# Loading part of one block without its padding rows: two 48-row transfers and engine fills in place of one 128-row transfer

## The chip, the cores and the metric

The kernel runs on one core of one Trainium2 chip. The metric is the device time of one execution in microseconds (us). The kernel before was timed in three runs: 544.09, 544.38 and 549.07 us, median 544.38 us. A further execution was recorded by the profiler; it took 545.84 us, of which 544.1 us lie between its first and its last instruction (the span).

## What is computed

An attention-like recurrence over four batches, eight heads, 768 steps and a head width of 48, and after it a dense layer with an elementwise function.

```
for t in range(S):                       # S = 768, heads of D = 48
    cur   = einsum('bhd,bhe->bhde', u * k[t], v[t])
    y[t]  = einsum('bhd,bhde->bhe', r[t], state + cur)
    state = w[t][:, :, :, None] * state + einsum('bhd,bhe->bhde', k[t], v[t])
x = y.transpose(0, 2, 1, 3).reshape(3072, 384)
h = x @ w_in                             # 384 x 2048
out = (h - tanh(h)) @ w_out              # 2048 x 384
```

## The kernel before, in words

The 3072 tokens are cut into eight blocks of 384 tokens (batch b, half q of the sequence). For each block the kernel first does the recurrence in chunks of 64 steps, and then the dense layer in 16 steps of 128 hidden columns. The recurrence of a block runs beside the dense layer of the block ahead of it; only the first block has nothing to run beside. It is done by the function boot (L1128), which stands at the very start. The change lies in boot alone.

Two heads share one tile of 128 rows: head 0 of a pair takes rows 0 to 47, head 1 takes rows 64 to 111, and rows 48 to 63 and 112 to 127 are padding (1.0 for w, 0.0 for k and r, from the host). There are four pairs. A block's half is two pairs: HALVES is (2, 0), so h1 is pairs 2 and 3, and h2 is pairs 0 and 1. The second half, h2, is what the change touches. For one half, w is a tile of 128 x 780 numbers (two pairs of six chunks of 65), k and r are 128 x 768. In the profile the tile of w of the first block is called states, since it lies in the buffer states0.

All loads of boot go out from one queue, SyncE's (SP), one after the other, through load (L361) and load_v (L401): w of pair 3, w of pair 2, k of h1, r of h1, w of h2, v of all four pairs, k of h2, r of h2, and then weights ("raw", 768 KB each, L251). The order on each engine is that in which the code is written, for PE, SP, VectorE (DVE) and ScalarE (ACT) alike (manual_schedule, L1102). Each transfer takes one of eight completion counters in turn, and in the emitted program a transfer waits until the one eight before it has landed.

What the steps of boot do, with the lines by which the profile names them:

- behind (L429) scans w backwards into post, before (L417) scans it forwards into pre; take_whole (L449) picks the decay of each chunk; both scans are on DVE.
- times_behind (L443, DVE) multiplies k into post; times_before (L436, DVE) multiplies r into pre; times_u (L454, ACT) multiplies k by u in place.
- own and earlier are gram products on PE (L494); their results are copied into the tile scores under a mask (L502, DVE). turn_1 (L517) transposes post on PE, turn_2 (L523, ACT) copies it out.
- update_half (L616, PE), states_half (L631, L632, DVE), from_scores (L697, PE), from_states (L679, PE) and result_out (L729) make the states and the block's result xT. The first dense step starts with L871 on PE.
- convert (L264 on ACT, L268 on DVE) makes fp32 weights of a raw tile.

On VectorE boot goes: behind and take_whole of h1, before, times_behind and times_before of h1, behind and take_whole of h2 (L429, L449), own of h1 (L502), times_behind of h2 (L443), earlier of h1 (L502), and so on. So the h2 scan L429 is the first user of w of h2, the L443 after it the first user of k of h2, and the second L436 the first user of r of h2.

Ahead of boot, VectorE fills the tiles shift (L152) and seed (L163, L164), GpSimd (POOL) makes ident and the tile start, which is 128 x 780 zeros (L171), and ScalarE copies zeros from start into scores (L205) and first_totals (L294). PE is kept busy with matmuls that nobody reads (L305, L312).

Of the kernel before, what the change touches and what calls it, by code (L numbers as in the profile page):

```python
# [50 lines left out]
B, H, S, D = 4, 8, 768, 48  # L51
P = 128
L = 64
NB = 384
NQ = S // NB
NCH = NB // L
NCP = NCH // 2
NPAIR = H // 2
LP = L + 1
WIDE = NPAIR * NCH * LP  # L60
HALF = WIDE // 2 + 2
UP = 2
# [64 lines left out]
def kernel(  # L127
# [12 lines left out]
    nc = tc.nc  # L140
# [29 lines left out]
    start = const.tile([P, UP * NCH * LP], F32, name="start", tag="start")  # L170
# [16 lines left out]
    def draw(names, cols):  # L187
        nc.gpsimd.memset(mask_all[0:L, cols], 1.0)
        for m in names:
# [5 lines left out]
            else:  # L195
# [10 lines left out]
                   in_=start[:, 0:BANK].unsqueeze(1).to_broadcast([P, 2 * NPAIR * NCP * L // BANK, BANK]))  # L206
# [46 lines left out]
    def convert(part, j, raw, _, tiles=1):  # L253

        lo, hi = raw[:, :, 0], raw[:, :, 1]
        a = w_sb[:, part, 2 * j:2 * j + 2].rearrange("p f c -> p (f c)").bitcast(I32)
        up = conv.tile([P, 2 * DM], I32, name="up", tag="up", bufs=4)
        low, high = (up.bitcast(t).rearrange("p (n two) -> p n two", two=2)[:, :, i]  # L260
                     for i, t in enumerate((U16, F16)))

        def scaled(to, of, scale, bias=0.0):
            return lambda: nc.scalar.activation(out=to, in_=of, func=AF.Copy, scale=scale, bias=bias)  # L264

        return [scaled(a.bitcast(F32), hi.bitcast(F32), HIGH_SCALE), scaled(high, hi.bitcast(F32), SIGN_SCALE),
                scaled(low, lo.bitcast(U32), *LOW)], [
                lambda of=slice(i * 2 * DM // tiles, (i + 1) * 2 * DM // tiles): nc.vector.scalar_tensor_tensor(  # L268
                    out=a[:, of], in0=a[:, of], scalar=3, in1=up[:, of], op0=ALU.logical_shift_left,
                    op1=ALU.bitwise_or) for i in range(tiles)]  # L270
# [43 lines left out]
    def begin_behind(ins, then):  # L314
        tc.add_manual_dep(then.ins, ins.ins.name, mybir.DependencyInfo(
            mybir.DependencyClass.Sync, mybir.DependencyReason.DATA))
# [3 lines left out]
    class Block:  # L320
# [37 lines left out]
                self.tot = work.tile([P, NPAIR * NCH], F32, name="whole", tag="whole")  # L358
            return self.tot[:, p0 * NCH:(p0 + n) * NCH]

        def load(self, name, p0=0, n=NPAIR, as_=None):  # L361
            as_ = as_ or name
            if name == "w":
                dst = self.tile(name)[:, p0 * NCH * LP:(p0 + n) * NCH * LP]
                src = wT[self.b, p0:p0 + n, :, self.q * NCH * LP:(self.q + 1) * NCH * LP]
            else:
                dst = self.tokens(as_, p0, n)
                src = {"r": rT, "k": kT}[name][self.b, p0:p0 + n, :, self.cols]
            return nc.sync.dma_start(out=dst.rearrange("d (p t) -> d p t", p=n),
                                     in_=src.rearrange("p d t -> d p t"))  # L370

        def by_token(self, name):

# [133 lines left out]
        def own(self, ps, p0, **fill):  # L507
            return self.masked(ps, "k", "r", masks["diagonal"], p0, **fill)

        def earlier(self, ps, p0, **fill):  # L510
            return self.masked(ps, "post", "pre", masks["above"], p0, **fill)
# [593 lines left out]
    def more_weights(queue):  # L1105
        raws.append(load_weights(more_weights.n, queue))
        more_weights.n += 1
        return raws[-1][-1]
# [3 lines left out]
    def run(ops):  # L1112
        for op in ops:
            op()
# [13 lines left out]
    def boot(ps, pair, blk, later):  # L1128
        h1, h2 = HALVES
        blk.tiles["w"] = states0  # L1130
        for name, p0, n in (("w", h1 + 1, 1), ("w", h1, 1), ("k", h1, UP), ("r", h1, UP), ("w", h2, UP)):
            blk.load(name, p0, n)
        blk.load_v()
        blk.load("k", h2, UP)
        blk.load("r", h2, UP)
        more_weights(nc.sync)

        both = (h1, h1 + 1), (h2, h2 + 1)
        blk.behind(h1 + 1, 1)
        blk.behind(h1, 1)  # L1140
        blk.take_whole(h1, UP)
        blk.totals_by_column(h1)
        nc.scalar.copy(out=later_ident, in_=ident)
        blk.before(h1, UP)
        blk.times_behind(h1, UP)
        blk.times_u(h1, UP)
        own = blk.own(ps, h1, spare=94, ahead=5, late=6)
        blk.turn_1(ps, h1)
        blk.times_before(h1, UP)
        earlier = blk.earlier(ps, h1)  # L1150
        blk.behind(h2, UP)
        blk.take_whole(h2, UP)
        first_a, first_b = convert(*raws.pop(0), tiles=2)
        own()
        blk.turn_2(h1)
        blk.totals_by_column(h2)
        blk.update_half(pair, h1)
        begin_behind(blk.done, more_weights(nc.sync))
        blk.times_behind(h2, UP)
        blk.times_u(h2, UP)  # L1160
        blk.turn_1(ps, h2)
        blk.turn_2(h2)
        earlier()
        blk.results(ps)
        blk.result("from_scores", both[0])
        run(blk.states_half(h1))
        blk.result("from_states", both[0], True, apart=True)
        blk.before(h2, UP)
        blk.update_half(pair, h2)
        blk.times_before(h2, UP)  # L1170
        own = blk.own(ps, h2)
        own_scored = blk.done
        run(first_a[:1])
        blk.result_out((3,), [nc.scalar.copy] * 2)
        blk.result_out((2,))
        earlier = blk.earlier(ps, h2, ahead=1)
        scored = blk.done
        onwards = blk.states_half(h2)
        own()
        run(first_a[1:])  # L1180
        needed = 2 * KC - 2
        blk.fill_holes([nc.sync, nc.gpsimd], range(needed, 2 * KC))
        begin_behind(own_scored, more_weights(nc.sync))
        blk.fill_holes([nc.sync, nc.gpsimd], range(needed))
        begin_behind(scored, more_weights(nc.sync))
        later.load("w")
        second_a, second_b = convert(*raws.pop(0))
        third_a, third_b = convert(*raws.pop(0))
        run(second_a)
        more_weights(nc.sync)  # L1190
        blk.results(ps)
        blk.yp.reverse()
        blk.result("from_states", both[1], apart=True)
        earlier(1, 1)
        earlier(0, 1)
        for p in reversed(both[1]):
            blk.result("from_scores", (p,), True, more=True)
        later.load("k")
        more_weights(nc.sync)
        run(onwards)  # L1200
        run(first_b[:1])
        for p in reversed(both[1]):
            blk.result_out((p,), [nc.scalar.copy, nc.vector.tensor_copy])
        run(first_b[1:])
        run(third_a[:2])
        run(second_b)
        blk.held(0, NPAIR)
        return [(third_a[2], third_b)]
# [6 lines left out]
    with tc.tile_pool(name="ps_boot", bufs=1, space=PSUM) as ps_boot:  # L1215
        pieces = boot(Turns([scratch(ps_boot)] + ps_a.both), [hp] + acc, blocks[0], blocks[1])
# [30 lines left out]
    for i, blk in enumerate(blocks):  # L1247
# [9 lines left out]
        for f in range(NF):  # L1257
# [60 lines left out]
            if not later and f == NF - 2:  # L1318
                at = n_whole + n_excess
# [29 lines left out]
            for name in loads.get(f, ()):  # L1349
                of, ins = (after if name in ("w", "k", "r") else later), None  # L1350
                if name == "weights":
                    ins = more_weights(nc.sync)
                elif name == "row":
                    ins = nc.sync.dma_start(out=u_row, in_=u_all)
                elif of and name.startswith("tokens"):
                    ins = of.load_tokens(name[-1])
                elif of:
                    ins = of.load_v() if name == "v" else of.load(name.split()[-1])
# [95 lines left out]
```

## Time and profile before

| what | value |
|---|---|
| three runs | 544.09, 544.38, 549.07 us |
| profiled execution, of that its span | 545.84 us, 544.1 us |
| VectorE, ScalarE busy | 459.0 us (84%), 403.8 us (74%) |
| DMA moved | 56.34 MB, mean 104 GB/s |
| mean granted TensorE clock | 0.995 |

The profile is one execution. Its page gives busy time per engine, and the chain of work that ended last, which is followed back from the last instruction. The timeline lists instructions by start (us from the span's start) and duration; a square bracket gives the idle time of the engine just before and what ended it. For a transfer the trace has the time of its issue on the queue and the time from the start of that issue until it has landed. The windows view gives for stretches of time the busy time of each engine, the granted TensorE clock, the mean busy share of the 16 DMA engines and what they moved.

### The profile page before, as it was taken

To read this page: it belongs to the slowest core of one execution; us is meant where nothing else is said; L and a number is where in the kernel's file an instruction comes from. 1 tells how busy PE (TensorE), PEld (TensorE's weight loads), DVE (VectorE), ACT (ScalarE), POOL (GpSimd) and SP (SyncE) were. 2 spreads that over 40 slices of the span, in tenths; PEclk is the share of its full clock that TensorE was granted. 3 is DMA by queue.
4 is the path that set the end of the run, shared out by engine and by line. 5 is a ranking of instruction groups with operands and counts; after the bars stand their busy time and mean duration, and the time that the engine had idled before them with its cause. 6 is when DMAs were issued, how large, how long until landed. Compare 5 with 4: busy or idle time off the path is not lost.

```text
span 544.1 us, 14866 instructions
## 1 busy us (share of the span) xinstructions
PE 533.7 (98%) x5682; PEld 404.1 (74%) x5682; DVE 459.0 (84%) x943; ACT 403.8 (74%) x814; POOL 6.6 (1%) x47
## 2 busy tenths in 40 slices
PE   7899999999999999999999999999999999999996
PEld 5756666678887788777877787877878787787874
DVE  7889999999989989789897979879897997457564
ACT  5799996888668876688676886588866885666561
POOL 1100000000000000000000000000000000000000
PEclk9899999999999999999999999999999999999999
DMA  7798633251402631154212532137231420200101
GB/s 274 236 400 308 237 102 115 87 146 60 121 19 79 159 110 54 58 128 138 60 55 73 121 116 67 49 89 161 67 97 54 92 56 2 57 1 0 45 1 46
DMA packets 53048, 56.34 MB, mean 104 GB/s; under 512 B 21488, under 2 KB 50928, under 8 KB 52976
## 3 DMA queue, kind: packets, MB, share of 16 engines
q1 hardware_dynamic: 52592, 55.18, 33.8%
q8 instruction: 48, 0.79, 0.6%
q14 instruction: 24, 0.20, 0.1%
q10 hardware_dynamic: 288, 0.10, 0.1%
q0 software_dynamic: 96, 0.07, 0.1%
HBM read 44.73 MB, written 4.72 MB: 91 GB/s over the span
## 4 chain that ended last, share of the span: by engine, by line
PE 95%; DVE 2%; issue 1%; DMA 0%; PEld 0%; PEldq 0%; DVEq 0%; SPq 0%
PE hp L871 44%; PE acc L999 26%; PE att L999 7%; PE acc L950 5%; PE att L757 4%; PE att L494 2%; PE acc L977 2%; PE att L575 1%; PE att L871 1%; PE acc L871 1%; DVE post L429 1%; DVE scores L502 1%; DMA states<-in_wT 0%; DVE pre L417 0%; PE att L977 0%
## 5 line engine op out<-in xcount | busy, mean ns | idle before, releaser
L871 PE MATMUL hp<-xT,w_sb 128*128 128x384 f32 x738 | 259.2, 487 | 0.4 <-DVE w_sb L268 0.4
L871 PEld LDWEIGHTS hp<-xT,w_sb 128*128 128x128 f32 x738 | 131.9, 190 | 69.7 <-issue 0.5
L999 PE MATMUL acc<-forms,g 128*128 128x128 f32 x954 | 133.2, 276 | 0.0
L876 ACT ACTIVATE h<-hp 128x384 f32<-128x384 f32 x123 | 60.4, 491 | 97.3 <-PE hp L871 97.1
L999 PEld LDWEIGHTS acc<-forms,g 128*128 128x128 f32 x954 | 122.0, 192 | 10.3
L879 DVE SCALAR_TENSOR_TENSOR h<-h,s 128x384 f32<-128x384 f32 x128 | 70.5, 551 | 50.5 <-ACT s L894 50.4
L920 DVE TENSOR_TENSOR g<-g 128x256 f32<-128x256 f32 x265 | 103.1, 418 | 7.3 <-PE acc L999 6.5
L895 ACT ACTIVATE qa<-s,shift 128x384 f32<-128x384 f32 x113 | 69.5, 615 | 3.7
L897 ACT ACTIVATE junk<-s,shift 128x384 bf16<-128x384 f32 x113 | 67.7, 599 | 0.0
L879 DVE SCALAR_TENSOR_TENSOR g<-qa,h 128x384 f32<-128x384 f32 x112 | 61.6, 550 | 1.6 <-ACT qa L905 0.2
L894 ACT ACTIVATE s<-h 128x384 f32<-128x384 f32 x113 | 59.1, 523 | 3.5
L999 PEld LDWEIGHTS acc<-w_sb,g 128*128 128x128 f32 x318 | 46.8, 191 | 9.7 <-ACT sums L967 0.3
L999 PE MATMUL acc<-w_sb,g 128*128 128x128 f32 x318 | 53.1, 276 | 0.0
L999 PE MATMUL att<-w_sb,g 128*128 128x128 f32 x212 | 35.5, 275 | 0.0
L999 PEld LDWEIGHTS att<-w_sb,g 128*128 128x128 f32 x212 | 31.1, 192 | 5.3
L1034 DVE TENSOR_TENSOR sums<-sums 128x256 f32<-128x256 f32 x84 | 32.8, 406 | 1.7 <-ACT sums L1011 1.5
L950 PE MATMUL acc<-w_sb,sums 128*128 128x384 f32 x96 | 33.7, 487 | 0.0
L264 ACT ACTIVATE up<-raw 128x768 f16<-128x768 f32 (+1 forms) x32 | 33.1, 1069 | 0.0
L950 PEld LDWEIGHTS acc<-w_sb,sums 128*128 128x128 f32 x96 | 18.0, 190 | 12.3 <-DVE sums L879 0.3
L417 DVE TENSOR_TENSOR_SCAN pre<-w,start 128x780 f32<-128x780 f32 x14 | 25.0, 1783 | 0.8
L429 DVE TENSOR_TENSOR_SCAN post<-w,seed 128x780 f32<-128x780 f32 x14 | 24.8, 1774 | 0.0
L897 ACT ACTIVATION_READ_ACCUMULATOR junk<-s,shift 128x1 f32 x113 | 21.1, 187 | 0.0
(118 smaller groups left out, 529.2 us busy)
## 6 DMA issues: line engine op xcount, KB each, us to landing
raw<-in_weights SPq DMA_DIRECT2D x16, 768.0 KB, 5.9
w<-in_wT SPq DMA_DIRECT2D x7, 780.0 KB, 4.6
k<-in_kT SPq DMA_DIRECT2D x7, 768.0 KB, 4.6
r<-in_rT SPq DMA_DIRECT2D x7, 768.0 KB, 4.6
v_sb<-in_v SPq DMA_DIRECT2D x8, 576.0 KB, 3.9
k<-in_tokens SPq DMA_DIRECT2D x7, 576.0 KB, 5.2
r<-in_tokens SPq DMA_DIRECT2D x7, 576.0 KB, 4.7
out_y<-sums SPq DMA_DIRECT2D x18, 128.0 KB, 1.8
```

Of the source, the lines that this page charges most:

```text
L264: return lambda: nc.scalar.activation(out=to, in_=of, func=AF.Copy, scale=scale, bias=bias)
L429: return nc.vector.tensor_tensor_scan(out=back(t[:, 0:width]), data0=back(self.tile("w")[:, a:a + width]), data1=back(seed[:, 0:width]), i ...
L871: nc.tensor.matmul(hp, lhsT=w_in_sb[:, f, kc, :], rhs=xT[kc], start=(kc == KC - 1), stop=(kc == 0))
L876: return h, nc.scalar.activation(out=h, in_=hp, func=AF.Copy, scale=1.0 / UPSCALE)
L879: return lambda: nc.vector.scalar_tensor_tensor(out=out, in0=in0, scalar=scalar, in1=in1, op0=op0, op1=ALU.mult)
L894: nc.scalar.activation(out=s, in_=h, func=AF.Square)
L895: nc.scalar.activation(out=qa, in_=s, func=AF.Square, bias=shift[:, 4:5])
L897: nc.scalar.activation(out=junk[:, 0:NB], in_=s, func=AF.Relu, bias=shift[:, 5:6], accum_out=excess[:, at:at + 1])
L920: return lambda: nc.vector.tensor_tensor(out=G[:, to:to + 2], in0=two(G, g_at(q, a0), g_at(q, a1)), in1=two(G, g_at(q, b0), g_at(q, b1)), ...
L950: nc.tensor.matmul(acc, lhsT=g[:, j * P:(j + 1) * P], rhs=w_out_sb[:, f, :], start=(f == self.first), stop=(f == NF - 1))
L999: nc.tensor.matmul(to, lhsT=G[:, g_at(q, a), :], rhs=rhs, start=start, stop=stop, skip_group_check=True)
L1034: ops.append(lambda op=op, at=at: nc.vector.tensor_tensor(out=at[0], in0=at[1], in1=at[2], op=OPS[op]))
```

## The change

load gets an argument rows, a list of row ranges, and issues one transfer for each. In boot, w, k and r of h2 are loaded for rows 0 to 47 and then for rows 64 to 111. The padding rows come from fills of the whole half tile, which are issued before these loads: w with 1.0 and k with 0.0 on VectorE, r on ScalarE by a copy from the tile of zeros. In the emitted program the fill of w stands on VectorE between the two fills of seed, the fill of k behind them and ahead of the first scan; the copy on ScalarE stands behind L294. Each of the first transfers of w, k and r waits for its fill.

```diff
-        def load(self, name, p0=0, n=NPAIR, as_=None):
+        def load(self, name, p0=0, n=NPAIR, as_=None, rows=(slice(0, P),)):
...
-            return nc.sync.dma_start(out=dst.rearrange("d (p t) -> d p t", p=n),
-                                     in_=src.rearrange("p d t -> d p t"))
+            for at in rows:
+                ins = nc.sync.dma_start(out=dst[at].rearrange("d (p t) -> d p t", p=n),
+                                        in_=src[:, at].rearrange("p d t -> d p t"))
+            return ins
...
     def boot(ps, pair, blk, later):
...
-        for name, p0, n in (("w", h1 + 1, 1), ("w", h1, 1), ("k", h1, UP), ("r", h1, UP), ("w", h2, UP)):
+        filled = slice(0, D), slice(64, 64 + D)
+        for name, p0, n in (("w", h1 + 1, 1), ("w", h1, 1), ("k", h1, UP), ("r", h1, UP)):
             blk.load(name, p0, n)
+        nc.vector.memset(blk.tile("w")[:, h2 * NCH * LP:(h2 + UP) * NCH * LP], 1.0)
+        nc.vector.memset(blk.tokens("k", h2, UP), 0.0)
+        nc.scalar.copy(out=blk.tokens("r", h2, UP), in_=start[:, 0:UP * NB])
+        blk.load("w", h2, UP, rows=filled)
         blk.load_v()
-        blk.load("k", h2, UP)
-        blk.load("r", h2, UP)
+        blk.load("k", h2, UP, rows=filled)
+        blk.load("r", h2, UP, rows=filled)
         more_weights(nc.sync)
```

## The prediction

> **What bounds the kernel now.** I read the page first, then the chain of work that ended last over the first 60 us, then the DMA issues of boot one by one, then the timeline of each engine there. The page's head:
>
> ```profile
> span 544.1 us, 14866 instructions
> PE 533.7 (98%) x5682; PEld 404.1 (74%) x5682; DVE 459.0 (84%) x943; ACT 403.8 (74%) x814; POOL 6.6 (1%) x47
> PE 95%; DVE 2%; issue 1%; DMA 0%; PEld 0%; PEldq 0%; DVEq 0%; SPq 0%
> ```
>
> TensorE bounds the run as a whole. All that the change touches lies before 25 us, in boot, and there the chain is another one:
>
> ```profile
> 0.94 2.60 DMA states<-in_wT
> 3.64 1.84 DVE post L429 x2
> ...
> 9.57 1.71 DVE post L429
> ...
> 11.39 0.66 DVE scores L502
> ...
> 12.31 0.16 DVE post L443
> ...
> 13.17 1.03 DVE scores L502
> 14.24 0.59 PEld att L697 x36
> ...
> 19.75 1.22 issue
> ...
> 25.02 4.98 PE acc L871 x12
> ```
>
> The chain waits for a transfer once, for the first piece of w, until 3.64 us. Then VectorE works without a gap, and the end of boot follows what it does; from 25.02 us on TensorE runs the dense steps. So what lies on this chain before 25 us moves the end by its full size, and what doesn't costs nothing. No step of the chain waits for w, k or r of h2: the first thing to say of the change is that it takes away no wait.
>
> How near are those transfers? Their issues on SP, and their times from issue to landing (each row below from a window that holds that issue):
>
> ```profile
> 2.33 0.48 SPq L369 DMA_DIRECT2D r<-in_rT  x1
> 2.85 0.47 SPq L369 DMA_DIRECT2D states<-in_wT  x1
> 3.37 0.48 SPq L406 DMA_DIRECT2D v_sb<-in_v  x1
> 3.89 0.76 SPq L369 DMA_DIRECT2D k<-in_kT  x1
> 4.69 0.92 SPq L369 DMA_DIRECT2D r<-in_rT  x1
> 5.65 8.21 SPq L251 DMA_DIRECT2D raw<-in_weights  x2
> ```
>
> ```profile
> r<-in_rT SPq DMA_DIRECT2D x1, 384.0 KB, 5.7
> ...
> states<-in_wT SPq DMA_DIRECT2D x1, 390.0 KB, 6.2
> ...
> v_sb<-in_v SPq DMA_DIRECT2D x1, 576.0 KB, 7.6
> k<-in_kT SPq DMA_DIRECT2D x1, 384.0 KB, 8.1
> ...
> r<-in_rT SPq DMA_DIRECT2D x1, 384.0 KB, 8.3
> ...
> raw<-in_weights SPq DMA_DIRECT2D x1, 768.0 KB, 9.2
> ```
>
> Issue plus landing: r of h1 8.03, w of h2 9.05, v 10.97, k of h2 11.99, r of h2 12.99, raw 14.85 us. Their first users:
>
> ```profile
> 9.49 1.77 DVE L429 TENSOR_TENSOR_SCAN post<-states,seed 128x780 f32<-128x780 f32 x1
> ...
> 12.31 0.94 DVE L443 TENSOR_TENSOR post<-k,post 128x768 f32<-128x768 f32 x1
> ...
> 17.88 0.96 DVE L436 TENSOR_TENSOR pre<-r,pre 128x768 f32<-128x768 f32 x1
> 14.98 0.90 ACT L264 ACTIVATE w_sb<-raw 128x768 f32<-128x768 f32 x1
> ```
>
> The margins are 0.44 us for w, 0.32 for k, 4.89 for r and 0.13 for raw. The second is the tight one: k lands 0.32 us ahead of a step of the chain, behind both w and v in the same stream.
>
> **The change, part by part.**
>
> *The fills on VectorE.* The fills of w (780 columns) and k (768) stand ahead of the first scan, between these rows and 3.64 us:
>
> ```profile
> 1.19 0.22 DVE L163 MEMSET seed<- 128x195 uint32 x1
> 1.52 0.07 DVE L164 MEMSET seed<- 128x12 uint8 x1
> ```
>
> The 195-column fill takes 0.22 us, 1.13 ns a column, so 0.88 and 0.87 us. From 1.41 us: 2.29, the small one to 2.36, the second to 3.23. The first w lands at 0.94 + 2.60 = 3.54, so 0.31 us are left: cost 0, hidden by the wait for the first w. By the 0.94 us that L443 takes over 768 columns they would end at 3.36, still hidden. Without that wait they would cost 1.75. Nothing on VectorE can be gained here.
>
> *The fill on ScalarE* stands behind L294:
>
> ```profile
> 2.74 1.46 ACT L205 COPY scores<-start 128x1536 f32<-128x1536 f32 x1
> 4.10 0.53 ACT L294 COPY first_totals<-start 128x192 f32<-128x192 f32 x1
> 5.71 0.59 ACT L623 COPY first_totals<-whole 128x480 f32<-128x480 f32 x1 [1.07 <-DVE whole L449]
> 5.81 0.23 DVE L416 RECIPROCAL start<-whole 128x12 f32<-128x12 f32 x1
> ```
>
> Half of L205's 1536 columns is 0.73 us, from 4.63 to 5.36 us. ScalarE was idle until 5.71. But L416 on VectorE overwrites a column of start, which the copy reads, so it must now wait for it: it begins at 5.81, 0.45 us later. Cost 0; beyond 0.45 us, each bit would be on the chain.
>
> *The queue SP.* w's first transfer waits for its fill (2.29 us; SP is there at 2.85), k's for 3.23 (SP: about 4.4), r's for 5.36. Three more issues at the 0.47 to 0.92 us above are 1.4 to 2.8 us, so SP reaches raw at 7.1 to 8.4 us instead of 5.65. The issue of raw also waits now for r of h1 (eight transfers earlier), which lands at 8.03. The DMA engines are then still busy with v, and its turn came only after r of h2, at 12.99: cost 0. The next raw waits for PE's L616 after 12 us, as before.
>
> *The transfers themselves* decide. Before, w, k and r of h2 land 1.02, 1.02 and 1.00 us behind what is ahead of them. Three rows from views by window: the rate from 10 to 12 us; the queue's packets, MB and share of 16 engines in a window of 5 us that holds a lone w load (126 to 131 us); the same for one that holds six copies of 16 rows from tile to tile (464 to 469 us, L777), the only transfers of few rows in the trace:
>
> ```profile
> 10.00:12.00 2.00, 2.00 (x78) 1.77 (x78) 1.97 (x3) 0.67 (x1) 0.00 (x0) 1.00 1.08 410
> ...
> q1 hardware_dynamic: 528, 0.80, 51.7%
> ...
> q1 hardware_dynamic: 189, 0.15, 12.5%
> ```
>
> The engines are full at 410 GB/s. A pair of 48-row transfers carries 96 of 128 rows. By bytes alone it takes 0.75 x 1.02 = 0.77 us; this is the low end. Yet each row still receives all its bytes, in two turns: if the time goes with the bytes of a row, and only half the rows take part in each, the pair takes 2 x 1.02 = 2.04 us, the high end. The lone w load moved 0.80 MB in 2.59 us of engine time, 309 GB/s; the 16-row transfers 0.15 MB in 0.63 us, 240 GB/s, 1.29 times as long per byte. At that ratio a pair takes 0.99 us, much as before. [...] I take the middle between 0.99 and 2.04, 1.5 us: 0.48 more for each of w, k and r.
>
> [...]
>
> *The sum.* w: 9.05 + 0.48 = 9.53, against 9.49: at most 0.04 late. k comes behind w and v: 11.99 + 0.96 = 12.95 against 12.31, 0.64 us late. Behind that L443 on VectorE wait L502, and for that PE's L697, and so the chain to 25.02. r: 12.99 + 1.44 = 14.43, against 17.88, hidden. raw: 16.29; ScalarE would be there at 14.98 + 0.64 = 15.62, so it loses some 0.7 us, most of which this idle time behind it takes up:
>
> ```profile
> 16.54 0.97 ACT L729 COPY late<-att 48x384 f32<-48x384 f32 x2 [0.66 <-PE att L679]
> ```
>
> So +0.64 us: 545.84 + 0.64 = 546.5 on the profiled execution. That one took 1.46 us more than the median of 544.38; against the median the forecast is **545.0 us**. By the ends: pairs of 0.77 and 0.99 give 0; 2.04 gives k at 14.03, 1.72 late, 546.1.
>
> **The rivals.**
>
> 1. *Nothing waits* (544.4 us). If a pair takes up to 1.18 us, k is late by no more than the 0.32 us that it has, and the change is off the chain. For it: the 16-row transfers at 0.99, and the bytes. Against it: the margin is a third of a microsecond, for two pairs in a row.
>
> 2. *The gap on PE goes away* (543.2 us; the side of a gain). The chain has 1.22 us of issue at 19.75, where PE waits for nothing that the profile shows, in the middle of L494. If that is PE's instructions coming late through the loaded DMA engines, fewer bytes or another order ahead of it could close it: 544.4 - 1.2. It decides if k is not late, or by less than the gap. Against it: from 18 to 20 us the DMA engines are busy for a quarter of the time only.
>
> ```profile
> 18.00:20.00 2.00, 1.75 (x86) 1.32 (x78) 2.00 (x3) 2.00 (x4) 0.89 (x2) 1.00 0.25 57
> 22.00:25.00 3.00, 2.76 (x85) 2.50 (x82) 1.48 (x6) 1.01 (x2) 0.00 (x0) 0.74 0.99 360
> ```
>
> 3. *The transfers use few engines* (about 550 us). If 48 rows are spread over 3 engines, 16 rows each, a pair runs at 3/16 of 410 GB/s, 77 GB/s: 300 KB in 3.9 us, 2.9 more each, k 5.8 later, less 0.32: +5.5. Against it: 48 is 16 x 3 as 128 is 16 x 8, and the 16-row transfers move 240 GB/s of busy time.
>
> 4. *The granted clock.* It is 0.74 from 22 to 25 us, after PE stood idle; up to 0.8 us of work is lost there. A later k leaves PE idle longer around 14 us and may shift this either way by about that much. It widens the range, and isn't a case by itself.
>
> **How the numbers follow.** k late by 0.1 to 1.7 us: 0.58. Nothing waits: 0.28. The gap goes: 0.07. Few engines: 0.04. A fill held too long, so that the first scan or L416 is late by a few tenths: 0.03. The range: from 544.4 less half a microsecond for the run to run spread, 543.9, to 546.1 plus 0.8 for the clock, 546.9. It leaves out the gap and the few engines, 0.11, and some of the edges. One per cent is 5.4 us, about what a measurement of this kernel can tell from no change. Only few engines reaches beyond it on the slow side (0.03 of 0.04), and only an unknown gain on the other (0.01), so within it 0.96.
>
> **What would show it.** In the profile after, L443 in boot begins 0.6 us later (12.9), with idle time on VectorE ahead of it that ends with the transfer of k; the first L871, at 25.0 before, begins later by as much; DMA windows between 8 and 14 us show fewer GB/s at a full share. If L443 begins at 12.3, rival 1 holds. If the first scan is later than 3.64 or L416 later than 5.81, a fill was not hidden. Wrong it would be if a pair takes less than 1.18 us, or if the issues on SP, not the engines, set when k arrives.

## The result, and the profile after

The kernel after takes 547.28 us (median of 22 runs, 545.51 to 552.00), the kernel before, run beside it, 544.46 us (22 runs, 543.87 to 549.07). The ratio is 1.006, with a 95% interval of 1.0044 to 1.0076: slower by 2.8 us, within the one per cent that the prediction calls no change, but 0.4 us beyond the top of its range (546.9).

The profiled execution of after took 548.99 us, its span is 547.3; the one of before has 544.1. The page's head, and its shares of the chain:

```profile
span 547.3 us, 14876 instructions
PE 535.0 (98%) x5682; PEld 404.1 (74%) x5682; DVE 460.9 (84%) x945; ACT 404.7 (74%) x815; POOL 6.6 (1%) x47
PE 89%; DVE 4%; DMA 3%; issue 1%; PEld 1%; ACT 0%; SPq 0%; PEldq 0%; DVEq 0%
```

PE has nearly the same work (535.0 us against 533.7), but DMA's share of the chain went from 0% to 3%. The chain over the first 60 us tells which transfers those are (start, duration, what):

```profile
0.94 2.51 DMA states<-in_wT
...
4.84 10.44 DMA k<-in_kT
15.41 0.97 DVE post L445
...
23.62 5.00 DMA xT<-late
28.76 1.65 PE acc L873 x4
```

The first wait, for the first piece of w, is the old one. The second is new: the second transfer of k of h2, issued at 4.84, lands at 15.28, and L445 (L443 before) begins behind it. The third, at 23.62, is new on the chain as well: it is a copy of 16 rows of the block's result, the tile xT, which the first dense step needs. Lines of after stand two higher from load on.

The issues on SP, and the times from issue to landing, each from a window that holds it:

```profile
2.86 0.94 SPq L370 DMA_DIRECT2D states<-in_wT  x2
3.84 0.43 SPq L408 DMA_DIRECT2D v_sb<-in_v  x1
4.39 1.27 SPq L370 DMA_DIRECT2D k<-in_kT  x2
5.76 0.98 SPq L370 DMA_DIRECT2D r<-in_rT  x2
8.68 0.35 SPq L251 DMA_DIRECT2D raw<-in_weights  x1
```

```profile
r<-in_rT SPq DMA_DIRECT2D x1, 384.0 KB, 6.3
states<-in_wT SPq DMA_DIRECT2D x1, 146.2 KB, 6.4
v_sb<-in_v SPq DMA_DIRECT2D x1, 576.0 KB, 10.4
k<-in_kT SPq DMA_DIRECT2D x1, 144.0 KB, 10.4
r<-in_rT SPq DMA_DIRECT2D x1, 144.0 KB, 10.0
raw<-in_weights SPq DMA_DIRECT2D x1, 768.0 KB, 9.4
```

So r of h1 (issued at 2.34) lands at 8.64, w of h2 at about 9.8, v at 14.24 (10.97 before), k at 15.28 (11.99), r of h2 at about 16.4 (12.99), raw at 18.08 (14.85). What VectorE did meanwhile:

```profile
1.52 0.71 DVE L1136 MEMSET states<- 128x780 f32 x1
...
2.38 0.70 DVE L1137 MEMSET k<- 128x768 f32 x1
3.55 1.99 DVE L431 TENSOR_TENSOR_SCAN post<-states,seed 128x390 f32<-128x390 f32 x2 [0.47 <-DMA states<-in_wT]
...
9.84 1.78 DVE L431 TENSOR_TENSOR_SCAN post<-states,seed 128x780 f32<-128x780 f32 x1
...
15.41 0.96 DVE L445 TENSOR_TENSOR post<-k,post 128x768 f32<-128x768 f32 x1 [2.65 <-DMA k<-in_kT]
```

The fills end at 3.08, ahead of the first w; the first scan still waits 0.47 us for that. The scan of h2 begins 0.35 us later than before (9.49), and L445 3.10 us later (12.31), after 2.65 us in which VectorE stood idle for k. The windows from 8 to 14 us of after, and the first of them of before (length, busy time of PE, PEld, DVE, ACT, POOL, granted clock, DMA share, GB/s):

```profile
8.00:10.00 2.00, 1.92 (x31) 0.67 (x29) 1.87 (x3) 1.12 (x2) 0.00 (x0) 1.00 1.08 272
10.00:12.00 2.00, 2.00 (x80) 1.76 (x78) 1.97 (x3) 0.59 (x1) 0.00 (x0) 1.00 1.12 229
12.00:14.00 2.00, 0.23 (x16) 0.09 (x8) 0.76 (x1) 0.69 (x2) 0.00 (x0) 1.00 1.09 227
```

```profile
8.00:10.00 2.00, 0.61 (x29) 0.53 (x32) 2.00 (x3) 1.12 (x2) 0.00 (x0) 1.00 1.05 381
```

The engines are as full as before (share 1.05 to 1.12), and move 227 to 272 GB/s where they moved 381 to 410. Fewer bytes go out, each at a higher price.

PE waits 2.15 us for v, until 14.38, where before has no wait, and 0.82 us for L445, until 16.42; from L445 the chain goes over the transposes of turn_1 (L519) to L699.

How it ends up in the time: the hp tile of the first dense step on PE, which began at 29.84 before and at 32.17 after (rows below), is 2.33 us late. In that lies a wait of 0.62 us for xT; on the other side before's execution has the gap of 1.22 us at 19.75 and a clock of 0.74 from 22 to 25 us and 0.54 from 25 to 27. From there to the 3.2 us by which the spans differ, 0.9 is missing: PE is busy for 24.27 us from 35 to 60 us where before had 24.55, and it stands idle for 0.5 us more behind 400 us.

```profile
29.84 2.10 PE L871 MATMUL hp<-xT,w_sb 128*128 128x384 f32 x6
```

```profile
28.76 3.57 PE L873 MATMUL acc<-xT,w_sb 128*128 128x384 f32 x10 [0.62 <-DMA xT<-late]
32.17 2.10 PE L873 MATMUL hp<-xT,w_sb 128*128 128x384 f32 x6
```

### The profile page after: what moved, and what is told of

It reads as the page before. It is cut to its first block, busy times and chain, and to the rows that moved or that the text cites. A ratio compares the mean times of both kernels' runs of the same rounds, so it can differ in the third digit from the quotient of the medians.

```text
span 547.3 us, 14876 instructions
## 1 busy us (share of the span) xinstructions
PE 535.0 (98%) x5682; PEld 404.1 (74%) x5682; DVE 460.9 (84%) x945; ACT 404.7 (74%) x815; POOL 6.6 (1%) x47
## 4 chain that ended last, share of the span: by engine, by line
PE 89%; DVE 4%; DMA 3%; issue 1%; PEld 1%; ACT 0%; SPq 0%; PEldq 0%; DVEq 0%
PE hp L873 43%; PE acc L1001 26%; PE att L1001 6%; PE acc L952 4%; PE att L759 4%; PE att L496 2%; DMA k<-in_kT 2%; PE acc L979 2%; PE att L577 1%; DMA xT<-late 1%; DVE w_sb L268 1%; DVE post L431 1%; DVE sums L881 1%; DVE s L904 1%; DVE post L445 1%
## 5 line engine op out<-in xcount | busy, mean ns | idle before, releaser
L952 PEld LDWEIGHTS acc<-w_sb,sums 128*128 128x128 f32 x96 | 17.9, 190 | 12.5 <-DVE sums L881 0.8
```

The costliest lines, as they stand in the source:

```text
L952: nc.tensor.matmul(acc, lhsT=g[:, j * P:(j + 1) * P], rhs=w_out_sb[:, f, :], start=(f == self.first), stop=(f == NF - 1))
```

## The experiments

The question is what made k 3.3 us later. The theories, by the letters that the expectations use: **A**, a transfer's time goes with the bytes of a row, not with the number of rows, so that two transfers of half the rows cost nearly twice one of all; bytes alone is the contrary; **B**, six transfers and their waits in the queue in place of three; **C**, the fills, and the waits for them on SP; **I**, the transfers delay also those that were issued ahead of them; **F**, its contrary, each pays only for what stands ahead; **T**, the granted TensorE clock, and **K**, that only the late k counts; **D** and **M**, a number of rows other than 128 is dear, wherever the rows lie (in the run with 64 rows D means 48 rows alone). The last of the small kernels tests M against another theory, that the time goes with which rows a transfer writes. Each run was profiled once, so a landing is one execution's: with whole loads k lands at 11.99 us before, at 12.4 with the fills alone and at 12.5 by columns.

**The fills alone.** The loads are whole again, 128 rows in one transfer, and still wait for the fills.

```diff
-        filled = slice(0, D), slice(64, 64 + D)
+        filled = slice(0, P),
```

> The three fills and the waits for them stay, but w, k and r of h2 come again in one transfer of 128 rows each. Theory A (transfers that touch only the rows of one half run at about half the rate of the stream, 1.9 us for a pair instead of 1.0, and this makes k late): as before, 544.5 us, first scan at 3.6 us, L443 of h2 (here L445) at 12.3 to 12.4 us. Theory C (the fills and the waits for them cost): slow as the changed kernel, 547 us, with an idle VectorE ahead of that step.

Measured: 544.34 us, ratio 1.0008 (0.9992 to 1.0025). On VectorE:

```profile
12.47 0.96 DVE L445 TENSOR_TENSOR post<-k,post 128x768 f32<-128x768 f32 x1 [0.16 <-DMA k<-in_kT]
```

L445 is 0.16 us later than before, and nothing of it reaches the end. Fills and waits cost nothing that can be measured; C falls. The profiled execution has a span of 542.4 us, and neither the 1.22 us of issue at 19.75 nor the clock of 0.74 that the one of before shows. Those belong to that execution, which fits its 1.46 us above the median. In this one the hp tile begins at 28.10:

```profile
28.10 2.10 PE L873 MATMUL hp<-xT,w_sb 128*128 128x384 f32 x6
```

Against it, after's hp tile is 4.07 us late, 2.94 us of that already at L445 (15.41 against 12.47).

**All rows, in halves.** No fills; rows 0 to 63 and rows 64 to 127, padding and all.

```diff
-        filled = slice(0, D), slice(64, 64 + D)
+        filled = slice(0, 64), slice(64, P)
...
-        nc.vector.memset(blk.tile("w")[:, h2 * NCH * LP:(h2 + UP) * NCH * LP], 1.0)
-        nc.vector.memset(blk.tokens("k", h2, UP), 0.0)
-        nc.scalar.copy(out=blk.tokens("r", h2, UP), in_=start[:, 0:UP * NB])
```

> No fills; w, k and r of h2 each in two transfers, rows 0 to 63 and rows 64 to 127, so all 128 rows and all bytes. Theory A: the pair takes as long as a pair of 48 rows or a little longer, about 1.9 to 2.1 us, k at about 15.3 us, 547 us. A theory by bytes or by number of pieces (D: 48-row transfers are slow because 48 rows spread badly over the engines): the pair takes 1.0 us, k at 12.0 us, 544.5 us.

Measured: 551.38 us (4 runs, 547.30 to 552.08), ratio 1.0106 (1.0061 to 1.0151).

```profile
11.26 1.78 DVE L431 TENSOR_TENSOR_SCAN post<-states,seed 128x780 f32<-128x780 f32 x1 [1.57 <-DMA states<-in_wT]
...
15.24 0.96 DVE L445 TENSOR_TENSOR post<-k,post 128x768 f32<-128x768 f32 x1 [1.07 <-DMA k<-in_kT]
```

Three of the four runs, the profiled one among them, had a mean clock of 0.982 to 0.984 and took 551.28 us and more; the fourth, at 0.997, took 547.30, so the median says little of the transfers. All bytes, in halves, are late by as much as 96 rows in halves (15.24 against 15.41), and w is later still. Bytes alone falls: a quarter fewer bytes bought nothing for k.

**As many transfers, cut the other way.** No fills; two transfers for each of w, k and r, of 128 rows and one pair of heads each.

```diff
-        blk.load("k", h2, UP, rows=filled)
+        for p in (h2, h2 + 1):
+            blk.load("k", p, 1)
```

(w and r likewise, and the fills removed.)

> No fills; w, k and r of h2 each in two transfers of 128 rows, one for each pair of heads. As many transfers as in the changed kernel, and the issue of raw waits for r of h1 as there. Theory A: no transfer touches half the rows only, so k lands at 12.0 us and the time is 544.5 us. Theory B (three more transfers on the queue, and the waits for the one eight before): k late as in the changed kernel, 547 us.

Measured: 545.19 us, ratio 1.0009 (0.9993 to 1.0025); L445 begins at 12.58, 0.27 us later than before. As many transfers, as many waits in the queue, and k is not 3 us late: B falls as the cause. That the time is the same is shown only to within the interval, which reaches 1.4 us.

**112 rows in one transfer.** The fills stay; rows 0 to 111 go in one.

```diff
-        filled = slice(0, D), slice(64, 64 + D)
+        filled = slice(0, 64 + D),
```

> The fills stay; w, k and r of h2 each in one transfer of rows 0 to 111: three transfers, 112 of 128 rows, 7/8 of the bytes. Theory A: rows of both halves in one transfer, so about the old rate, k at 11.7 to 12.3 us, 544.5 us. Theory D (a number of rows other than 128 spreads badly over the engines): k late by over 1 us, 546 us or more.

Measured: 546.70 us, ratio 1.0035 (1.0014 to 1.0056).

```profile
14.94 0.96 DVE L445 TENSOR_TENSOR post<-k,post 128x768 f32<-128x768 f32 x1 [2.59 <-DMA k<-in_kT]
```

By A one transfer of 112 rows had to be as good as one of 128. It isn't: k lands at 14.87, nearly as late as by halves, with seven eighths of the bytes. A misses here, and what D expected came: there is something about other shapes than 128 rows that isn't the halving.

This execution also shows how the late k reaches the end, for its clock is 1.00 up to 100 us and its PE does not wait for xT:

```profile
30.63 2.10 PE L873 MATMUL hp<-xT,w_sb 128*128 128x384 f32 x6
```

Against the execution with the fills alone, L445 is 2.47 us late, the hp tile 2.53 (28.10 there), and the span 2.7 us longer (545.1 against 542.4). The late k is passed on at its full size.

**Each pair alone.** In turn only r, only k, only w of h2 goes in two transfers with its fill; the other two are whole. For r:

```diff
-        nc.vector.memset(blk.tile("w")[:, h2 * NCH * LP:(h2 + UP) * NCH * LP], 1.0)
-        nc.vector.memset(blk.tokens("k", h2, UP), 0.0)
...
-        blk.load("w", h2, UP, rows=filled)
+        blk.load("w", h2, UP)
...
-        blk.load("k", h2, UP, rows=filled)
+        blk.load("k", h2, UP)
```

> Only r of h2 in two transfers of 48 rows, with its fill; w and k whole, as before. r stands behind v and k on the queue. Theory F (a transfer delays itself and what is behind it): v and k land as before, L445 of h2 at 12.3 to 12.5 us, 544.5 us. Theory I (the transfers run into each other, so that slow ones behind also hold up what was issued ahead): v or k later by 0.3 to 1 us, 544.8 to 545.5 us.

> Only k of h2 in two transfers of 48 rows, with its fill; w and r whole. By the pair time of about 1.9 us that the changed kernel and the run with 112 rows point to (1.0 before): k about 0.9 us later than before, L445 of h2 at about 13.0 us, 545.1 us. If theory I holds, v later than 11 us too. If the cost is in the number of transfers or in the waits: as before, 544.5 us.

> Only w of h2 in two transfers of 48 rows, with its fill; k and r whole. Theory F with a pair time of 1.9 us: w, v and k each about 0.9 us later, the h2 scan (L431) at 10.0 us instead of 9.5, L445 at 12.9 to 13.1 us, 545.1 us. Theory I: r of h1, ahead of it, also lands later than 8.0 us.

Measured: r alone 545.96 us (1.0023, 1.0006 to 1.0040), k alone 545.74 (1.0021, 1.0005 to 1.0037), w alone 545.53 (1.0018, 1.0006 to 1.0030). The three add up to 0.62%, where all three at once cost 0.60%; each of these figures is uncertain by about 0.15. Here L445 with r alone and the scan of w with k alone:

```profile
13.46 0.96 DVE L445 TENSOR_TENSOR post<-k,post 128x768 f32<-128x768 f32 x1 [0.97 <-DMA k<-in_kT]
```

```profile
10.05 1.78 DVE L431 TENSOR_TENSOR_SCAN post<-states,seed 128x780 f32<-128x780 f32 x1 [0.53 <-DMA states<-in_wT]
```

These are the two lines that matter. With r alone, all that stands ahead of k in the queue is as before, and r is issued behind k; yet k lands at 13.39, 1.40 us later than before and 1.0 later than with the fills alone. With k alone, w stands ahead of it, and lands 0.53 us after VectorE is ready for it: its scan now begins at 10.05 in place of 9.49, and of 9.40 with the fills alone. So the transfers aren't served one after the other: one that goes badly also delays those ahead of it that have not landed yet. F falls, I holds, on one execution of each of two kernels. With w alone, r of h1, ahead of w, lands at 8.3, against 7.1 to 8.1 with whole loads (three executions); that is too little to tell.

**PE kept busy.** After, with 8 matmuls that nobody reads before update_half of h1, and 3 ahead of turn_1 of h2, to keep PE from standing idle for v and k.

```diff
...
+        busy(pair[0], 8)
         blk.update_half(pair, h1)
...
-        blk.turn_1(ps, h2)
+        blk.turn_1(ps, h2, ahead=3)
```

> The changed kernel with eleven more matmuls that nobody reads, where TensorE waits in it: eight ahead of the first update_half (it waits there for v), three ahead of the second turn_1. Theory T (a good part of the 0.6% is the TensorE clock, which falls after the waits to 0.5 to 0.6, and the spread of the times comes from it): granted clock 1.00 from 14 to 30 us, times closer together, about 546.0 us. Theory K (only the late k counts): 547 us with the same spread as before it, whatever the clock. If the filler itself delays: 547.5 us or more.

Measured: 548.38 us (6 runs, 547.82 to 549.54), ratio 1.0074 (1.0057 to 1.0092). From 16 to 18 us, after:

```profile
16.00:18.00 2.00, 1.58 (x10) 1.25 (x14) 2.00 (x4) 1.12 (x2) 0.00 (x0) 0.54 0.56 159
```

and with PE kept busy:

```profile
16.00:18.00 2.00, 1.65 (x57) 1.30 (x56) 1.97 (x4) 2.00 (x4) 0.00 (x0) 1.00 0.95 261
```

The clock stays at 1.00 where after has 0.54, and the median is no better. That doesn't clear the clock, for what PE gains is lost again: L682 on PE (L681 in after) begins at 17.88 in place of 19.71, but then PE waits 1.66 us for xT, whose last copies stand in SP's queue behind a load of raw issued at 21.33, and the hp tile begins at 31.61, only 0.56 us earlier than in after.

```profile
27.64 4.14 PE L874 MATMUL acc<-xT,w_sb 128*128 128x384 f32 x12 [1.66 <-DVE xT L732]
```

The loads are those of after to the last transfer, and yet L445 begins earlier here:

```profile
14.73 0.96 DVE L445 TENSOR_TENSOR post<-k,post 128x768 f32<-128x768 f32 x1 [2.41 <-DMA k<-in_kT]
```

So two executions of the same loads differ by 0.68 us, and what is said of k in single executions holds no finer than that: the 3.3 us may be 2.2 (14.6 for k here, 12.4 with the fills alone).

What the clock is worth, the runs by themselves show better. The nine of after's 22 runs at a mean clock of 0.998 to 1.000 took 545.5 to 547.4 us, median 546.70; the four at 0.982 to 0.990 took 549.3 to 552.0. Of before, 47 runs beside three of these experiments (the fills alone, r alone, r last) had 0.998 to 1.000 as well, median 544.25. So by this comparison some 2.4 of the median's 2.8 us are there at an almost full clock, and the spread goes with the clock: with PE kept busy all six runs are at 0.995 or more and lie within 1.8 us. T accounts for the spread and for a small part of the median.

**r last.** r's two transfers are issued behind the first weights.

```diff
-        blk.load("r", h2, UP, rows=filled)
         more_weights(nc.sync)
+        blk.load("r", h2, UP, rows=filled)
```

> The changed kernel with the two transfers of r of h2 issued after the first tile of raw instead of ahead of it. Theory I (slow transfers hold up those issued ahead of them): a raw tile of 128 rows now follows k, so k lands up to 1 us earlier than in the changed kernel, L445 of h2 at about 14.3 to 14.8 us instead of 15.4, 546.3 us. Theory F (a transfer delays only what is behind it): v and k as in the changed kernel, L445 at 15.4 us, 547.2 us.

Measured: 547.73 us (547.23 to 551.66), ratio 1.0067 (1.0044 to 1.0091). L445 begins at 14.66, 0.75 us earlier than after, which is what I expects, but hardly earlier than the 14.73 that the same loads as after's gave with PE kept busy. So it speaks neither for I nor for F. The time is no better; the profiled execution has a clock of 0.50 from 16 to 30 us, and the three runs at 0.997 and more took 547.2 to 547.7.

**The price of a shape by itself.** Three kernels leave out all of the kernel's work: they load pieces of r into tiles, group by group, and write zeros. The instructions in a group go out one behind the other from SP, and VectorE reads one column of each tile before the next group starts. In the first, a group is four turns of one shape. (A group's line names the tile that is read behind the arrow; the last figures are VectorE's wait for it.)

```diff
+    group("whole", [(sp, slice(0, P), both)])
+    group("fortyeight", [(sp, slice(0, 48), both)])
+    group("fortypair", [(sp, slice(0, 48), both), (sp, slice(64, 112), both)])
...
+    group("sixtypair", [(sp, slice(0, 64), both), (sp, slice(64, P), both)])
+    group("hundredtwelve", [(sp, slice(0, 112), both)])
```

> None of the kernel's work is done here: the kernel only loads pieces of r into tiles of zeros, in groups of four tiles, each group after all of the one ahead has landed, and writes zeros as its result. Each group takes 2 to 2.5 us of latency and its transfers. Bytes alone (theory of the low end): four tiles of 128 rows 4.0 us more, of 48 rows 1.5, of 48-row pairs 3.0, of 64 rows 2.0, of 112 rows 3.5. Theory A (half of the rows, half of the rate): 48 and 64 rows about 4.0, the pairs about 8, 112 and 96 rows about 4. Theory M (any transfer of other than 128 rows shares rows between engines and is slowed): 112 and 96 rows about 8, 48 and 64 rows about 4, pairs about 8; two halves of the columns as 128 rows. Two queues for the two halves at once: 8 if they still stand behind each other, 4 if they run side by side.

```profile
L42 DVE COPY sixtyfour<-fortypair 128x1 f32<-128x1 f32 x4 | 0.6, 154 | 6.7 <-DMA fortypair<-in_rT 6.7
L42 DVE COPY hundredtwelve<-sixtypair 128x1 f32<-128x1 f32 x4 | 0.6, 154 | 8.5 <-DMA sixtypair<-in_rT 8.5
...
L42 DVE COPY ninetysix<-hundredtwelve 128x1 f32<-128x1 f32 x4 | 0.6, 154 | 7.0 <-DMA hundredtwelve<-in_rT 7.0
...
L42 DVE COPY fortyeight<-whole 128x1 f32<-128x1 f32 x4 | 0.6, 152 | 6.1 <-DMA whole<-in_rT 6.1
```

Against four whole ones, four pairs of 48 take 0.6 us more, 0.15 each; four pairs of 64 take 2.4 more, 0.60 each; four of 112 rows take 0.9 more, 0.23 each, with fewer bytes. Four of 96 rows take as long as four whole ones (6.1), four of 120 rows 1.9 more (8.0). Four single transfers of 48 rows took 5.1 us, a pair with its halves on two queues 6.4, no way out, and four loads cut in two by columns 6.7, as much as the pairs of 48. So A misses: it expected the pairs to take some 4 us more than whole ones. 0.15 is far from what a pair cost in boot.

In the second kernel each of four turns is a whole load and then the shape, as in boot, where v and others stand between.

```diff
+    group("plain", [whole])
+    group("wholes", [whole, whole])
+    group("withpair", [whole, (sp, slice(0, 48), both), (sp, slice(64, 112), both)])
...
+    group("withtwelve", [whole, (sp, slice(0, 112), both)])
```

> None of the kernel's work is done here: only loads of r in groups, each after the one ahead has landed, and zeros as the result. Each of four turns loads one whole tile of 128 rows, and after it: nothing; another whole tile; a pair of 48 rows; a pair of 64 rows; 48 rows once; two halves of the columns; 112 rows. Among their own kind a whole tile took 0.98 us, a 48-row pair 1.13, a 64-row pair 1.59, 112 rows 1.23. If the price is a transfer's own, the groups take 4 x 1.13, 4 x 1.59 and 4 x 1.23 us more than four whole tiles, beside 4 x 0.98 for a whole one. If it comes from the change between shapes, a 48-row pair and 112 rows take about 4 x 2.0 us more, as the kernel's runs point to.

```profile
L41 DVE COPY withpair<-wholes 128x1 f32<-128x1 f32 x8 | 1.2, 154 | 10.7 <-DMA wholes<-in_rT 10.6
...
L41 DVE COPY wholes<-plain 128x1 f32<-128x1 f32 x8 | 1.2, 153 | 6.2 <-DMA plain<-in_rT 6.1
L41 DVE COPY withsixty<-withpair 128x1 f32<-128x1 f32 x8 | 1.2, 153 | 12.7 <-DMA withpair<-in_rT 12.6
L41 DVE COPY withtwelve<-withcolumns 128x1 f32<-128x1 f32 x8 | 1.2, 153 | 10.0 <-DMA withcolumns<-in_rT 9.9
...
L60 DVE COPY done<-withtwelve 128x1 f32<-128x1 f32 x8 | 1.0, 150 | 12.6 <-DMA withtwelve<-in_rT 12.6
```

Over the plain group's 6.1 us, a whole one adds (10.6 - 6.1) / 4 = 1.12 us, a pair of 48 (12.6 - 6.1) / 4 = 1.63, and one of 112 rows as much. A load cut in two by columns adds 0.95, a pair of 64 rows (13.5 in all) 1.85, and rows 0 to 47 alone (10.0) 0.98. Between whole loads a pair costs 0.5 us more than the whole load that it replaces, against 0.15 among its own kind. That fits a price for the change between shapes, but each group was loaded once and lands unevenly: two neighbours among the whole loads lie 2.3 us apart where most lie 1.0, worth 0.3 us in a turn.

In the third kernel the shapes differ by where the rows lie, seven transfers each.

```diff
+    group("lowhalf", [(sp, slice(0, 64), both)])
+    group("middle", [(sp, slice(32, 96), both)])
...
+    group("lowdata", [(sp, slice(0, 48), both)])
+    group("acrossdata", [(sp, slice(40, 88), both)])
```

> None of the kernel's work is done here: only groups of seven loads of r of one kind, each group after the one ahead has landed, and zeros as the result. Groups: 128 rows; rows 0 to 63; 32 to 95; 64 to 127; 48 to 111; 0 to 31; 0 to 47; 40 to 87. [...] Theory M (any number of rows other than 128 is slow, wherever the rows lie): 0.9 for each group of 64 rows and 0.74 for both of 48.

The reads of three groups on VectorE, one line for each that starts when a transfer has landed: two of the whole loads; the first and the sixth of rows 0 to 47; the first and the last, which is the seventh, of rows 40 to 87:

```profile
60.33 0.15 DVE L41 COPY lowhalf<-whole 128x1 f32<-128x1 f32 x1 [0.93 <-DMA whole<-in_rT]
61.39 0.15 DVE L41 COPY lowhalf<-whole 128x1 f32<-128x1 f32 x1 [0.90 <-DMA whole<-in_rT]
...
106.68 0.15 DVE L41 COPY acrossdata<-lowdata 128x1 f32<-128x1 f32 x1 [2.99 <-DMA lowdata<-in_rT]
...
111.51 0.15 DVE L41 COPY acrossdata<-lowdata 128x1 f32<-128x1 f32 x1 [0.80 <-DMA lowdata<-in_rT]
...
114.79 0.15 DVE L60 COPY done<-acrossdata 128x1 f32<-128x1 f32 x1 [2.40 <-DMA acrossdata<-in_rT]
...
118.37 0.15 DVE L60 COPY done<-acrossdata 128x1 f32<-128x1 f32 x1 [0.44 <-DMA acrossdata<-in_rT]
```

A whole load of 384 KB takes 1.06 us here (1.12 on average over all seven). One of rows 0 to 47, 144 KB, takes (111.51 - 106.68) / 5 = 0.97 us, nearly as long. As many bytes in rows 40 to 87 take (118.37 - 114.79) / 6 = 0.60 us on average. Rows 0 to 63 come 0.99 us apart, rows 32 to 95 0.72. So in these groups of 48 and 64 rows it isn't the number of rows, nor the bytes of a row, but above all which rows: rows 0 to 47 are nearly as dear as all 128. M misses in that: it expected 0.9 us for each group of 64 rows and 0.74 for both of 48. But not every range across row 64 is cheap: rows 48 to 111 come 0.95 us apart. What it is in the rows that sets the time, no run shows. Two transfers in turn at the 0.97 us of rows 0 to 47, 1.93, would be close to what a pair cost in boot (an estimate: rows 64 to 111 were not loaded alone); yet among their own kind, in the first of these kernels, four pairs took 6.7 us in place of the 6.1 of four whole loads, not twice as long. So that the price in boot comes from this is argued, not shown.

## Why the prediction was wrong

**What was right.** No wait was taken away, and none is missing from the chain. Fills: predicted 0.88 and 0.87 us on VectorE, measured 0.71 and 0.70, hidden by the first w as said; on ScalarE, predicted 0.73 and measured as here, ahead of the next instruction:

```profile
4.43 0.84 ACT L1138 COPY r<-start 128x768 f32<-128x768 f32 x1
```

It ends at 5.27; L418 on VectorE (L416 before) begins at 5.88 in place of 5.81. Issues on SP cost nothing by themselves that can be measured: the run by columns has as many, and a ratio of 1.0009 (0.9993 to 1.0025). k was the tight one, and the loss comes through L443, now L445, as forecast (from there over L519 on PE, not L502); the engines show a full share (1.08 to 1.12) at fewer GB/s (227 to 272). Rival 1 (nothing waits) is out with L445 at 15.41. Rival 2 (the gap on PE goes away) is out as a cause: the gap of 1.22 us is missing also where only the fills were added; why one execution has it stays open. Rival 3 (few engines) is out by its size: pairs cost about 1.9 us, not 3.9.

**Wrong, first: "I take the middle between 0.99 and 2.04, 1.5 us".** From the landing of r of h1 to that of r of h2, before took 12.99 - 8.03 = 4.96 us, after some 16.4 - 8.64 = 7.8. Less 1.92 for v, as it took before (10.97 - 9.05), three pairs took 5.9 us, nearly 2.0 each. Other executions give a range: r of h2 lands at 13.0 to 13.5 with whole loads (before, the fills alone, by columns), at 16.4 in after and at 15.6 with PE kept busy, so that each of the three pairs cost 0.7 to 1.1 us more than the whole load of 1.0, 1.7 to 2.1 us. That is near the high end, all the bytes of a row at the price of the whole load. The low side of the middle came from the 16-row copies, 1.29 times as long per byte; those were the wrong row to go by: they say nothing of rows 0 to 47, of which a transfer by itself took 0.97 us, with 1.06 for a whole load. The middle itself was the author's estimate: no run shows 1.5 for a pair, and boot showed 1.7 to 2.1.

**Wrong, second: "k comes behind w and v: 11.99 + 0.96 = 12.95".** The sum let k pay for its own pair and w's, 2 x 0.48, as if the stream were served in order. It isn't: r's pair alone, issued behind k, made k 1.0 to 1.4 us later. So k paid for three pairs, and v, which the prediction never charged, came 3.27 us later (14.24 against 10.97), with PE waiting for it. Had the sum charged the high end for all three, 3 x (2.04 - 1.02) = 3.06 us, k would have been at 15.05, 2.74 late against 12.31, and the forecast 544.4 + 2.7 = 547.1, next to the 547.28 measured. That it comes so close is in part luck: the same loads had L445 at 14.73 with PE kept busy, and the measured median holds some clock and the wait for xT as well. Mending only the first leaves k at 14.03, only the second at 13.43; it takes both.

**Wrong, third: what is late next.** The prediction ended at L871. raw is 3.2 us later too (18.08), but ScalarE comes to it only at 18.70. The last copies of xT stand in SP's queue behind a later load of raw, which is issued at 23.16 in place of 18.87, when the gram products of h2 (L496) are done on PE; so they are issued at 23.62 in place of 19.97, and PE waits 0.62 us for them. And the clock has more than the 0.8 us allowed for: runs of after reach 552.00.

What stays open: why rows 0 to 47 take 0.97 us and as many bytes in rows 40 to 87 0.60; why 112 rows in one transfer, and 120, are slower than 128 (0.23 and, (8.0 - 6.1) / 4, 0.48 us each); how much of boot's 1.7 to 2.1 us is the halves and how much the change between shapes (0.15 more than a whole load among pairs, 0.5 more between whole loads, 0.7 to 1.1 in boot); and why the clock falls in some executions of a kernel and not in others. No version here beats before: nothing waited for these transfers, so there was nothing to gain from them, and the best of them, the fills alone and the two halves by columns, only equal it within their intervals.

## What to carry to other kernels

Before leaving out rows of a load, ask whether anything waits for it, and which rows are left: two transfers of 48 rows, 0 to 47 and 64 to 111, never cost less here than the one whole load, 0.15 us more among their own kind and 0.7 to 1.1 more in boot, though they have a quarter fewer bytes; where a load must be cut, cut it by columns, which left L445 here at 12.58 us, against 15.41 in after. In a loaded queue charge a dear transfer to all that is in flight, ahead of it too (r's pair put k, issued ahead of it, back by 1.0 to 1.4 us), and look at the one with the smallest margin, here 0.32 us. Where the nearest row for a price is of another shape, the middle of the range has nothing behind it: load the shape itself in a small kernel, and among the transfers that it will stand between. And before a difference in one trace is read, look what the same loads do in another: here 0.68 us.

## What the runs showed of the hardware that was not expected

- Rows 0 to 47 (144 KB) took 0.97 us, rows 40 to 87 (144 KB) 0.60 and rows 48 to 111 (192 KB) 0.95, beside 1.06 for all 128 (384 KB).
- Two transfers delayed those issued ahead of them on the same queue: r's pair, behind k, put k back by 1.40 us and v by 0.90 (11.87 against 10.97); against the execution with the fills alone it is 1.0 and 0.5 us (12.4 and 11.4 there).
- One transfer of 112 rows took 0.23 us more than one of 128, and in boot three of them put k back by 2.9 us (14.87 against 11.99).
- A fill of 128 x 780 fp32 numbers took 0.71 us on VectorE, 0.91 ns a column, where the 195-column fill of the seed took 1.13.
